# Layer 2's ELU goes through h's PSUM bank: g's two parts taken from there, and the order planned anew

## The chip, the cores and the metric

One Trainium2 chip, one core. The time is the device time of one execution in microseconds (us), on the slowest core, which here is the only one; lower is better. TensorE (PE), its weight loads (PEld), VectorE (DVE), ScalarE (ACT), GpSimd (POOL) and SyncE's DMA queue (SP) run beside each other and wait for one another by semaphores.

## What is computed

Three stages follow each other: an attention with hashed buckets, and two layers of a feed-forward network on its output.

```python
q_bucket, k_bucket = ...            # 6 sign bits of q @ proj, k @ proj
scores = scale * (q @ k.T), -1e9 where the buckets differ
attn = exp(scores - max) / (sum + 1e-9)
x = attn @ v                        # 16 heads x 768 x 64 -> 1536 tokens x 512
h = x @ w_in                        # layer 1, 512 -> 2048
g = h * tanh(softplus(h))           # Mish
x = g @ w_out                       # 2048 -> 512
h = x @ w2_in                       # layer 2, the same sizes
g = where(h > 0, h, exp(min(h, 0)) - 1)   # ELU
out = g @ w2_out
```

The weights reach the chip as 64 bit patterns and are turned into fp32 pairs there. Every product of the layers is made of three: each operand is split into a high part in fp32r and a low part, what is left, and high x high, high x low and low x high are summed in PSUM.

## The kernel before

**Attention.** 96 steps, 16 heads by 6 tiles of 128 queries. A step computes scores on PE (`st`), masks and takes the maximum on DVE (`pt`, L651), the exponential on ACT (L656), transposes on PE (`tu`, L707), splits the transposed part into `pth` (ACT, L712) and `ptl` (DVE, the helper `sub`, L353), and multiplies by v (`xt`, L720).

**Layers.** Tokens are columns: three blocks of 512 (`c` = 0, 1, 2). A layer is 32 tiles of weights (`w0` to `w31` and `w32` to `w63`; `u` counts them), in the order of `unit_orders`. "Up" products write h of one block into one PSUM bank, 12 matmuls each; "down" products read four tiles g and are added into `y_acc`, by ACT or by DVE (L1202). The first four up tiles are computed plainly (in layer 2: `h32_*` to `h35_*`), then the first down tiles follow (`h36_0`, `h37_0`, `h36_2` and so on, which read `g32` to `g35`, in this order). The other up tiles come in pairs, by seven products instead of eight (`pair_step`): results `h38_b1` to `h38_b4` for the outer blocks, and `h38_1c` and `h38_2c` for the middle one, each a bank; ACT copies `p` and DVE's additions at L957 join them. `turn` makes the sums of x that the pairs need, in `y_acc`, `T`, `x_hi` and `x_lo` (L1040 and the helpers), once for each layer, at its start; each of its additions and subtractions may run on DVE or on POOL.

**From h to g.** Each up tile goes from its bank to g, with `g.tile[:, 0]` its high part and `g.tile[:, 1]` its low part. Layer 1 (`mish`): ACT applies Mish in the bank, and `split` casts g's high part from the bank (ACT, the helper `copy`, L348) and subtracts it there (DVE, `sub`, L353). Layer 2 (`elu`, L893 to L904) has five instructions: relu of -h into a tile `gg` in SBUF (ACT, L896), the exponential of -gg in place (ACT, L898), max(gg - 1, h) into gg (DVE, L900), the cast of gg (ACT, L348) and the subtraction (L353), on DVE or POOL as the plan finds. The tiles `gg` are a ring of two (`NGG`).

**Weights.** `convert` turns a raw tile `wraw` into a weight pair: an ACT cast (L396), DVE's four instructions L398 (into a bank of their own, `c`), L401, L415, L418, and a cast and two or three sums and differences on ACT and POOL (L348, L353, L423, L432). In the attention the first ones run without that bank (L405, L410, L413, L415 on DVE). Seven PSUM banks go round among the h tiles, one belongs to `c`.

**What sets the order.** Nothing is scheduled by hand or while running: `Plan` lists every operation with a cost per engine, its inputs, its buffers and a priority, and gives each engine its sequence; the program then issues the instructions in that order. PE's sequence in the layers is fixed by the list of steps. Buffers of a ring are handed on in the plan's order. Tables of numbers (`EDGE`, `SHIFT`, `OFF`, `ODD`) shift the priorities of single operations; `pool` and `pool2` are the costs of an operation on POOL.

Of the kernel before, what the change touches and what calls it, by code (L numbers as in the profile page):

```python
# [30 lines left out]
def unit_orders():  # L31
# [25 lines left out]
EDGE = {}  # L57
SHIFT = {
# [78 lines left out]
def dve(n, fast=False):  # L137
    return 75 + (0.514 if fast else 1.028) * n


def act(n, psum=True):
    return (52 if psum else 95) + 0.833 * n


def pool(n):
    return 150 + 2.22 * n


def pool2(n):
    return 150 + 2.38 * n  # L150
# [144 lines left out]
def kernel(ctx, tc, qk, v, w, tab, out):  # L295
# [20 lines left out]
    def f32(t):  # L316
        return t.bitcast(F32)
# [983 lines left out]
```

## Time and profile before

| | |
|---|---|
| median of 3 runs | 739.52 us (739.17 to 742.06) |
| the profiled execution | 742.38 us, its span 740.6 us |
| granted clock of TensorE | 1.00 in all of the span (the 2.4 GHz level) |
| PE busy | 727.1 us, 98% |
| DVE busy | 579.4 us, 78% |
| ACT busy | 490.4 us, 66% |
| POOL busy | 423.2 us, 57% |
| time in the attention | to about 235 us, the layers from there on; layer 2 from about 480 us |

The page's busy times tell which engine can be the bound, the view of waits whom it waited for, and the timeline of a stretch what each engine did there, with the idle time ahead of a row and who ended it in square brackets. Line numbers are those of the kernel before; behind the change they are one higher up to the function `elu` and one lower behind it (L353 is L354 then, L900 is L901, L1040 is L1039).

### The profile page before, as it was taken

Reading aid. Unit: us, or ns where it says so; the run is one execution under the profiler, and the core shown is the slowest. Engines: PE = TensorE matmul, PEld = TensorE weight load, DVE = VectorE, ACT = ScalarE, POOL = GpSimd, SP = SyncE. Lnnn points to the kernel's source line nnn. Section 1 sums busy time; section 2 is a strip of 40 time slices with the busy share of each in tenths; the row PEclk is TensorE's granted clock in tenths of the full one; section 3 lists DMA queues with packets and bytes.
Section 4 is the critical chain, followed back from the end, with each engine's and each line's share of the span. In section 5 each row is a group of like instructions: output and inputs, shape, how many; then the busy total and the mean of one; then the engine's idle time right before and its main releaser. Section 6 shows DMA issues by size and latency. Waiting matters only on the chain. (4 is left out here: it accounts for less than half of the span.)

```text
span 740.6 us, 11709 instructions
## 1 busy us (share of the span) xinstructions
PE 727.1 (98%) x4083; PEld 639.0 (86%) x4083; DVE 579.4 (78%) x1065; ACT 490.4 (66%) x977; POOL 423.2 (57%) x359
## 2 busy tenths in 40 slices
PE   8999999999999999999999999999999999999998
PEld 7999999999898887888888888887788888888887
DVE  6899999999998979486577668999766785866672
ACT  5998998989997666554273457467766754844740
POOL 5427735734637886446446536866664755765640
PEclk9999999999999999999999999999999999999999
DMA  6875867777620302122112202212121121121112
GB/s 191 206 187 150 204 176 178 190 175 184 143 61 29 114 30 70 44 86 85 58 58 74 98 30 86 86 57 81 34 86 58 58 86 58 58 85 58 58 72 99
DMA packets 27498, 72.93 MB, mean 98 GB/s; under 512 B 6048, under 2 KB 8240, under 8 KB 27440
## 3 DMA queue, kind: packets, MB, share of 16 engines
q1 hardware_dynamic: 27296, 72.17, 34.3%
q8 instruction: 32, 0.52, 0.3%
q14 instruction: 26, 0.21, 0.1%
q10 hardware_dynamic: 144, 0.01, 0.0%
HBM read 45.76 MB, written 3.19 MB: 66 GB/s over the span
## 5 line engine op out<-in xcount | busy, mean ns | idle before, releaser
L848 PE MATMUL h<-g,w 128*128 128x512 f32 x1140 | 267.1, 390 | 3.0 <-DVE g L353 3.0
L848 PEld LDWEIGHTS h<-g,w 128*128 128x128 f32 x1140 | 212.6, 188 | 48.0 <-DVE g L353 4.1
L353 DVE TENSOR_TENSOR ptl<-tu,pth 128x512 fp32r<-128x512 f32 x144 | 97.5, 687 | 7.4 <-ACT pth L712 5.0
L651 DVE TENSOR_SCALAR_CACHE_REDUCE pt<-st 128x768 f32<-128x768 f32 x96 | 90.6, 948 | 5.7 <-PE st L648 5.4
L656 ACT ACTIVATE pt<-pt,nb 128x768 f32<-128x768 f32 x96 | 90.7, 945 | 3.6 <-DVE nb L654 3.4
L712 ACT CAST pth<-tu 128x512 fp32r<-128x512 f32 x144 | 82.2, 582 | 13.6 <-PE tu L707 12.7
L707 PE MATMUL tu<-ident,pt 128*128 128x128 f32 x576 | 85.9, 275 | 2.9 <-DVE ptl L353 2.8
L353 POOL TENSOR_TENSOR wt<-wt,w 128x512 f32<-128x512 f32 x40 | 52.8, 1320 | 62.1 <-DVE c L415 39.4
L1202 DVE TENSOR_TENSOR y_acc<-h,y_acc 128x512 f32<-128x512 f32 x71 | 48.8, 687 | 50.3 <-PE h L848 50.2
L648 PE MATMUL st<-qkt 76*128 76x384 f32 (+1 forms) x384 | 86.7, 350 | 0.8 <-DVE pt L651 0.8
L720 PE MATMUL xt<-pth,vt 128*128 128x256 f32 x288 | 79.3, 304 | 0.0
L707 PEld LDWEIGHTS tu<-ident,pt 128*128 128x128 f32 x576 | 67.4, 140 | 10.4 <-DVE ptl L353 6.2
L720 PE MATMUL xt<-ptl,vt 128*128 128x256 f32 x288 | 72.7, 281 | 0.0
L648 PEld LDWEIGHTS st<-qkt 76*128 76x128 f32 (+1 forms) x384 | 63.8, 191 | 1.7 <-DVE pt L651 1.7
L848 PE MATMUL h<-x_hi,w 128*128 128x512 f32 x192 | 60.5, 390 | 0.0
L348 ACT CAST w<-wt 128x512 fp32r<-128x512 f32 (+1 forms) x64 | 37.2, 583 | 33.0 <-DVE wt L401 18.0
L423 POOL TENSOR_TENSOR wt<-wt,ws 128x512 f32<-128x512 f32 x24 | 31.9, 1328 | 42.5 <-DVE ws L418 42.0
L432 POOL TENSOR_TENSOR w<-wt,ws 128x512 fp32r<-128x512 f32 x40 | 53.4, 1335 | 4.6 <-DVE ws L418 2.2
L720 PEld LDWEIGHTS xt<-ptl,vt 128*128 128x128 f32 x288 | 54.7, 190 | 0.1
L720 PEld LDWEIGHTS xt<-pth,vt 128*128 128x128 f32 x288 | 54.4, 189 | 0.0
L398 DVE TENSOR_SCALAR c<-ws 128x512 int32<-128x512 int32 x61 | 42.0, 689 | 14.3 <-ACT ws L396 12.7
L350 POOL CAST z<-rw 128x768 fp32r<-128x768 f32 x14 | 11.6, 826 | 64.0 <-DMA qkt<-z 41.7
(151 smaller groups left out, 1549.8 us busy)
## 6 DMA issues: line engine op xcount, KB each, us to landing
wraw<-in_w_dram SPq DMA_DIRECT2D x64, 512.0 KB
qkt<-z SPq DMA_DIRECT2D x30, 384.0 KB
rw<-in_qk_dram SPq DMA_DIRECT2D x16, 384.0 KB
qkt<-z SPq DMA_DIRECT2D x31, 192.0 KB
vr<-in_v_dram SPq DMA_DIRECT2D x8, 384.0 KB
out_dram<-y_acc SPq DMA_DIRECT2D x11, 256.0 KB
rr<-dr SPq DMA_DIRECT2D x14, 192.0 KB
xs<-xr SPq DMA_DIRECT2D x14, 192.0 KB
```

What stands on the lines that cost most here:

```text
L348: nc.scalar.copy(out=out, in_=in_)
L353: eng(e).tensor_tensor(out=out, in0=a, in1=b, op=ALU.subtract)
L398: o2 = p.op({DVE: dve(n)}, lambda e: nc.vector.tensor_scalar(out=bits(b), in0=bits(a), scalar1=3, scalar2=None, op0=ALU.logical_shift_left ...
L432: o9 = p.op({POOL: cost}, lambda e: nc.gpsimd.tensor_tensor(out=lo(), in0=t.tile, in1=s.tile, op=ALU.add), [o6, o8], [t, s, w_], prio)
L648: nc.tensor.matmul(st.tile[:, c, 0:HS], lhsT=wt.tile[0:n, q, t * 128:(t + 1) * 128], rhs=wt.tile[0:n, 2 + q, c * HS:(c + 1) * HS], start=( ...
L651: o = max_op = p.op({DVE: dve(S)}, lambda e: nc.vector.tensor_scalar(out=half(pt.tile), in0=st.tile[:, :, 0:HS], scalar1=-MASKED / SCALE, ...
L656: o = p.op({ACT: act(S, False) + 196}, lambda e: nc.scalar.activation(out=pt.tile, in_=pt.tile, func=AF.Exp, bias=nb.tile, scale=SCALE, ac ...
L707: nc.tensor.transpose(tu.tile[:, k, j], pt.tile[:, (2 * b + k) * 128:(2 * b + k + 1) * 128], ident)
L712: o = p.op({ACT: act(512)}, lambda e, tu=tu, ks=ks: nc.scalar.copy(out=hi.tile[:, ks], in_=flat(tu)), [o], [tu, hi], order(i, 'hi'))
L720: nc.tensor.matmul(xt.tile[:, 0:TH], lhsT=vt.tile[:, k, g % 2], rhs=m.tile[:, k], start=(k == 0 and j == 0), stop=(k == NKT - 1 and j == 1))
L848: nc.tensor.matmul(out(), lhsT=w_.tile[:, a, k], rhs=r, start=(start and n == 0), stop=(stop and n == 3 * len(ks) - 1), skip_group_check=True)
L1202: y = p.op({DVE: dve(n)}, lambda e, ya=ya, t=t, c=c: nc.vector.tensor_tensor(out=ya, in0=view(t.tile, c), in1=ya, op=ALU.add), [x, Y[m, c] ...
```

## The change

The maximum at L900 writes back into h's bank instead of gg; what follows is layer 1's `split`: the cast reads the bank (ACT), the subtraction reads the bank and runs on DVE. The two cost functions of POOL are given one new line, and the tables hold new numbers, so the whole order is planned anew.

```diff
-EDGE = {}
+EDGE = {'rr5': -12.0, 'rh#1': -1.0, ...
 SHIFT = {
-    'P1#0': -28, 'P1#1': -25.25, 'P1.1': -5, 'P1c#0': -20.5, 'P1c#1': 3.5, 'P1c.1': -22.75, 'P2#0': 19.5,
+    'P1#0': 41.25, 'P1#1': -121, 'P1.1': 37.5, 'P1c#0': 28.5, 'P1c#1': 53.75, 'P1c.1': -46.5, 'P2#0': -49.25,
...
 def pool(n):
-    return 150 + 2.22 * n
+    return 140 + 2.185 * n
 def pool2(n):
-    return 150 + 2.38 * n
+    return 140 + 2.185 * n
...
             a = p.op({DVE: dve(n)}, lambda e: nc.vector.scalar_tensor_tensor(
-                out=gg.tile, in0=gg.tile, scalar=1.0, in1=t.tile, op0=ALU.subtract, op1=ALU.max), [a], [t, gg], prio)
-            h = p.op({ACT: act(n, False)}, lambda e: copy(e, g.tile[:, 0], gg.tile), [a], [gg, g], prio)
-            return p.op({DVE: dve(n), POOL: pool2(n)} if BOTH else {POOL: pool2(n)}, lambda e: sub(
-                e, g.tile[:, 1], gg.tile, f32(g.tile[:, 0])), [h], [gg, g], prio, port=True)
+                out=t.tile, in0=gg.tile, scalar=1.0, in1=t.tile, op0=ALU.subtract, op1=ALU.max), [a], [t, gg], prio)
+            return split(t, a, prio, g)
```

**What moves between engines.** PE has 4085 instructions and ACT 884 in both; DVE goes from 971 to 986, POOL from 364 to 349. Layer 2's 48 subtractions were 22 on DVE and 26 on POOL and are all on DVE. Of the turns' work some goes the other way: of the 256 wide sums into `y_acc` DVE has 7 instead of 15, of the subtractions into `T` 15 instead of 20, of the 512 wide ones into `y_acc` 12 instead of 13, of those into `x_lo` 4 instead of 1. PE's order is the same in both layers; in the attention it differs for about steps 7 to 20 and for its last 30 us. The conversions of w0 and w1 that the attention hides are placed otherwise among DVE's rows: L410 of w0 three rows earlier, L415 of w1 eleven rows later.

**DVE, the start of layer 2, around g35_0's low part.** `gg...` is the ELU's buffer of the tile named behind it, `c39`, `wt39` and `ws39` are stages of the conversion of w39. Before:

```order
L900 SCALAR_TENSOR_TENSOR gg1252_6184<-gg1252_6184,h34_2_6146 128x512
L900 SCALAR_TENSOR_TENSOR gg1245_6171<-gg1245_6171,h35_0_6120 128x512
L398 TENSOR_SCALAR c39_6212<-ws39_6162 128x512
L401 SCALAR_TENSOR_TENSOR wt39_6217<-wraw39_6108,c39_6212 128x512
L415 TENSOR_SCALAR c39_6212<-wt39_6217 128x512
L418 SCALAR_TENSOR_TENSOR ws39_6162<-wraw39_6108,c39_6212 128x512
L353 TENSOR_TENSOR g34_2_6215<-gg1252_6184,g34_2_6215 128x512
L353 TENSOR_TENSOR g35_0_6219<-gg1245_6171,g35_0_6219 128x512
```

and of the change:

```order
L901 SCALAR_TENSOR_TENSOR h34_0_6109<-gg1238_6146,h34_0_6109 128x512
L402 SCALAR_TENSOR_TENSOR wt39_6160<-wraw39_6078,c39_6153 128x512
L416 TENSOR_SCALAR c39_6153<-wt39_6160 128x512
L354 TENSOR_TENSOR g34_0_6172<-h34_0_6109,g34_0_6172 128x512
L901 SCALAR_TENSOR_TENSOR h35_0_6136<-gg1245_6175,h35_0_6136 128x512
L419 SCALAR_TENSOR_TENSOR ws39_6150<-wraw39_6078,c39_6153 128x512
L354 TENSOR_TENSOR g35_0_6188<-h35_0_6136,g35_0_6188 128x512
```

The maximum writes h35_0's bank, one instruction of w39 stands between it and the subtraction instead of four, and g34_2 comes behind.

**ACT, the same place.** Before:

```order
L896 ACTIVATE gg1245_6171<-h35_0_6120 128x512
L896 ACTIVATE gg1252_6184<-h34_2_6146 128x512
L898 ACTIVATE gg1245_6171<-gg1245_6171 128x512
L348 CAST T1_0_3699<-y_acc_3696 128x256
L898 ACTIVATE gg1252_6184<-gg1252_6184 128x512
L348 CAST T2_0_3701<-y_acc_3696 128x256
L348 CAST x_hi_64<-y_acc_3696 128x512 x2
L348 CAST g34_2_6215<-gg1252_6184 128x512
L348 CAST g35_0_6219<-gg1245_6171 128x512
```

and of the change:

```order
L897 ACTIVATE gg1245_6175<-h35_0_6136 128x512
L899 ACTIVATE gg1245_6175<-gg1245_6175 128x512
L349 CAST T0_1_3698<-y_acc_3696 128x256
L349 CAST g35_0_6188<-h35_0_6136 128x512
L897 ACTIVATE gg1252_6201<-h34_2_6162 128x512
L349 CAST T1_1_3700<-y_acc_3696 128x256
L899 ACTIVATE gg1252_6201<-gg1252_6201 128x512
```

The tile's relu, exponential and cast stand with one other cast between them, and the next tile's relu behind its cast.

**DVE, the first pair of layer 2 (w38, w39), at its joined middle results.** Before:

```order
L900 SCALAR_TENSOR_TENSOR gg1405_6675<-gg1405_6675,h38_1c_6554 128x512
L398 TENSOR_SCALAR c45_6697<-ws45_6692 128x512
L900 SCALAR_TENSOR_TENSOR gg1412_6677<-gg1412_6677,h38_2c_6565 128x512
L401 SCALAR_TENSOR_TENSOR wt45_6712<-wraw45_6515,c45_6697 128x512
L415 TENSOR_SCALAR c45_6697<-wt45_6712 128x512
L418 SCALAR_TENSOR_TENSOR ws45_6692<-wraw45_6515,c45_6697 128x512
L353 TENSOR_TENSOR g38_1_6715<-gg1412_6677,g38_1_6715 128x512
```

and of the change:

```order
L901 SCALAR_TENSOR_TENSOR h38_1c_6556<-gg1405_6670,h38_1c_6556 128x512
L901 SCALAR_TENSOR_TENSOR h38_2c_6566<-gg1412_6676,h38_2c_6566 128x512
L399 TENSOR_SCALAR c44_6702<-ws44_6695 128x512
L354 TENSOR_TENSOR g39_1_6697<-h38_1c_6556,g39_1_6697 128x512
L354 TENSOR_TENSOR g38_1_6704<-h38_2c_6566,g38_1_6704 128x512
```

Both subtractions are DVE's now (g39_1's was POOL's) and stand behind one instruction of w44. The bank of h38_1c goes to h42_1c in both.

## Rows read from the trace of the kernel before

**Rows 1.** The page, busy time of each engine (share of the span) and instructions.

```profile
PE 727.1 (98%) x4083; PEld 639.0 (86%) x4083; DVE 579.4 (78%) x1065; ACT 490.4 (66%) x977; POOL 423.2 (57%) x359
```

**Rows 2.** Waits of PE: who waited for whom, us in total, times, longest.

```profile
PE h L848 <- DVE g L353: 3.0, 3, 1.4
PE tu L707 <- DVE ptl L353: 2.8, 3, 1.0
...
PE h_b L848 <- ACT p L348: 0.8, 1, 0.8
```

**Rows 3.** Busy time by stretch: length; PE, PEld, DVE, ACT, POOL; PEclk, DMA share, GB/s.

```profile
500.00:540.00 40.00, 37.35 (x163) 30.02 (x162) 32.69 (x49) 28.91 (x55) 25.26 (x21) 1.00 0.20 66
540.00:735.00 195.00, 195.00 (x977) 165.51 (x977) 130.99 (x205) 107.78 (x200) 113.19 (x98) 1.00 0.20 68
```

**Rows 4.** Timeline of PE, start of layer 2: start, us, instructions, [idle before, releaser].

```profile
518.34 5.75 PE L848 MATMUL h<-g,w 128*128 128x512 f32 x24 [1.29 <-DVE g L353]
525.45 1.90 PE L848 MATMUL h<-g,w 128*128 128x512 f32 x7 [1.36 <-DVE g L353]
```

**Rows 5.** Timeline of ACT, the same place.

```profile
508.72 1.08 ACT L896 ACTIVATE gg<-h 128x512 f32<-128x512 f32 x2
...
513.03 1.14 ACT L348 CAST g<-gg 128x512 fp32r<-128x512 f32 x2
516.70 0.60 ACT L896 ACTIVATE gg<-h 128x512 f32<-128x512 f32 x1 [2.54 <-DVE g L353]
```

**Rows 6.** Timeline of DVE, the same place.

```profile
515.92 2.36 DVE L353 TENSOR_TENSOR g<-gg,g 128x512 fp32r<-128x512 f32 x2
...
523.04 2.35 DVE L353 TENSOR_TENSOR g<-gg,g 128x512 fp32r<-128x512 f32 x2
```

**Rows 7.** Timeline of POOL, the same place.

```profile
516.08 1.66 POOL L423 TENSOR_TENSOR wt<-wt,ws 128x512 f32<-128x512 f32 x1 [0.84 <-DVE ws L418]
```

**Rows 8.** Groups of instructions, shapes apart: count | busy, mean ns of one | idle before.

```profile
L353 POOL TENSOR_TENSOR g<-gg,g 128x512 fp32r<-128x512 f32 x26 | 33.5, 1298 | 14.6 <-ACT g L348 14.6
L898 ACT ACTIVATE gg<-gg 128x512 f32<-128x512 f32 x48 | 30.4, 633 | 0.9
...
L957 DVE TENSOR_TENSOR h_b<-h_b,p 128x512 f32<-128x512 f32 x36 | 25.1, 696 | 14.1 <-PE h_b L848 11.0 <-ACT p L348 3.1
L353 DVE TENSOR_TENSOR g<-gg,g 128x512 fp32r<-128x512 f32 x22 | 20.6, 954 | 3.1 <-ACT g L348 2.7
L900 DVE SCALAR_TENSOR_TENSOR gg<-gg,h_b 128x512 f32<-128x512 f32 x24 | 16.5, 686 | 12.8 <-ACT gg L898 11.3 <-POOL w L432 1.5
L353 DVE TENSOR_TENSOR g<-h_b,g 128x512 fp32r<-128x512 f32 x24 | 16.5, 686 | 7.6 <-ACT g L348 7.6
...
L348 ACT CAST g<-h_b 128x512 fp32r<-128x512 f32 x24 | 14.2, 594 | 0.5 <-PE h L848 0.3
```

**Rows 9.** Timelines of POOL, DVE and PE in the attention, around 57 and 197 us.

```profile
54.88 1.84 POOL L757 TENSOR_TENSOR xr<-xr,xs 128x768 f32<-128x768 f32 x1
...
55.27 2.00 DVE L410 SCALAR_TENSOR_TENSOR wt<-wraw,wt 128x512 int32<-128x512 int32 x1
...
57.93 0.66 PE L707 MATMUL tu<-ident,pt 128*128 128x128 f32 x4 [0.98 <-DVE ptl L353]
...
194.61 1.98 DVE L415 TENSOR_SCALAR ws<-wt 128x512 int32<-128x512 int32 x1
...
197.70 0.66 PE L707 MATMUL tu<-ident,pt 128*128 128x128 f32 x4 [1.04 <-DVE ptl L353]
```

**Rows 10.** Timelines of DVE and PE where banks change hands, layer 1 and layer 2.

```profile
298.13 0.69 DVE L353 TENSOR_TENSOR g<-h_b,g 128x512 fp32r<-128x512 f32 x1
...
298.87 1.45 PE L848 MATMUL h<-g,w 128*128 128x512 f32 x5 [0.39 <-DVE g L353]
...
566.52 0.69 DVE L900 SCALAR_TENSOR_TENSOR gg<-gg,h_1c 128x512 f32<-128x512 f32 x1
...
569.53 0.28 PE L848 MATMUL h_1c<-x_hi,w 128*128 128x256 f32 x1
```

More of the change, by code (lines that the diff above doesn't have):

```diff
@@ L56 @@
 SEED, SPREAD = 0, 0.0
-EDGE = {}
+EDGE = {'rr5': -12.0, 'rh#1': -1.0, 'rh#2': -4.0, 'rh#3': 3.75, 'rh#13': -10.5, 'rh#14': 31.5, 'cp#1': 5.5, 'cp#3': 1.5, 'cp#14': -5.25, 'cp#15': 19.75, 'ld#1': -16.0, 'ld#2': -11.75, 'ld#13': -4.0, 'ld#14': 19.0, 'ld#15': 14.5, 'sp#1': -27.0, 'sp#2': -1.25, 'sp#13': -7.5, 'sp#14': -15.5, 'sp#15': -10.75, 'pj#2': -2.75, 'pj#3': -2.5, 'bits#2': -7.0, 'bits#3': -43.75, 'bits#13': 8.0, 'pc#2': 25.75, 'pc#3': 4.5, 'pc#13': 8.0, 'pc#14': -7.25, 'pc#15': -37.0, 'pb#1': -1.25, 'pb#2': 18.75, 'pb#3': 66.5, 'mk#1': 14.5, 'mk#2': 8.0, 'mk#3': 3.75, 'mk#13': -29.0, 'mk#14': 22.0, 'S0': 1.0, 'S1': 0.5, 'S2': 1.25, 'S4': 14.75, 'S6': -29.25, 'S7': -37.5, 'S8': -8.75, 'S9': -14.25, 'S10': -15.5, 'S87': -0.25, 'S88': 2.5, 'S90': 26.75, 'S91': 8.5, 'S92': -1.0, 'S94': 16.25, 'S95': 17.0, 'max0': -9.5, 'max1': 42.25, 'max2': 10.5, 'max3': -16.0, 'max5': -3.0, 'max6': 2.5, 'max7': -0.5, 'max8': 24.25, 'max9': 1.75, 'max10': -0.25, 'max11': -25.0, 'max12': -2.0, 'max84': -25.0, 'max85': 12.5, 'max86': 15.0, 'max87': -7.75, 'max88': 3.5, 'max89': -21.75, 'max93': -0.25, 'max94': -22.75, 'max95': 20.25, 'exp2': -1.75, 'exp3': -18.75, 'exp4': -8.5, 'exp5': -0.5, 'exp6': 14.5, 'exp7': 57.75, 'exp9': 2.0, 'exp10': 12.5, 'exp11': -3.0, 'exp12': -2.5, 'exp13': -11.25, 'exp86': -31.75, 'exp87': 4.0, 'exp88': -23.25, 'exp89': 3.0, 'exp90': 11.0, 'exp91': -0.25, 'exp92': -2.5, 'exp93': 7.0, 'exp94': 11.25, 'exp95': -11.0, 'sum5': -24.0, 'sum11': 1.5, 'sum87': 29.25, 'sum89': -7.0, 'sum93': 17.75, 'sum95': 6.5, 'eps5': -0.25, 'eps11': -4.75, 'eps85': -8.25, 'eps87': 14.75, 'eps89': -9.25, 'eps91': -20.25, 'eps93': -6.5, 'eps95': 48.0, 'T1': -12.75, 'T3': 10.75, 'T5': -29.75, 'T7': 28.75, 'T9': 7.75, 'T11': -8.0, 'T13': 1.0, 'T85': 8.75, 'T87': -21.75, 'T89': 8.5, 'T91': 8.0, 'T93': -0.5, 'T95': -11.5, 'hi3': 12.0, 'hi5': -0.25, 'hi7': 3.75, 'hi11': -63.0, 'hi13': -2.25, 'hi85': 21.25, 'hi87': 10.0, 'hi89': -10.25, 'hi91': 36.25, 'hi93': 4.25, 'hi95': 16.25, 'lo1': 3.75, 'lo3': -5.25, 'lo5': 13.5, 'lo7': 2.0, 'lo9': -8.75, 'lo11': -39.0, 'lo13': 4.0, 'lo85': -0.25, 'lo89': 27.25, 'lo91': -1.75, 'lo93': 17.0, 'lo95': -10.75, 'R91': -2.75, 'R93': -3.0, 'R95': 0.25, 'pv1': -4.25, 'pv11': 0.25, 'pv13': -0.25, 'pv85': 1.0, 'pv87': 11.5, 'pv91': 24.0, 'pv93': 11.75, 'pv95': 24.75, 'xc1': 19.0, 'xc3': -9.25, 'xc5': -52.75, 'xc7': -1.5, 'xc13': 3.75, 'xc85': -0.75, 'xc87': 42.75, 'xc89': -3.5, 'xc93': -0.5, 'xm5': -8.0, 'xm11': 8.0, 'rr11': 10.0, 'rh#15': 21.0, 'cp#2': 5.75, 'cp#13': 9.25, 'ld#3': -3.0, 'sp#3': 15.5, 'pj#1': -1.75, 'pj#13': 0.25, 'bits#1': -6.25, 'bits#14': 14.5, 'S13': -2.0, 'S86': 2.25, 'S89': 0.5, 'S93': 17.0, 'max4': 27.0, 'max91': -36.75, 'exp84': -2.0, 'sum85': 7.0, 'hi1': -16.25, 'hi9': -12.25, 'pv3': -1.75, 'pv5': -2.0, 'pv7': -0.25, 'pv9': 0.5, 'pv89': -28.25, 'xn11': 4.0}
@@ L131 @@
 WAIT = {'PE': 150, 'ACT': 0, 'DVE': 50, 'POOL': 50, 'SP': 100}
-OFF = {'rr': 41.5, 'rh': 63.5, 'cp': -137.25, 'ld': 2.0, 'sp': -1.25, 'pj': -5.75, 'bits': -149.5, 'pc': 18.0, 'pb': -54.0, 'mk': 208.25, 'v': 55.25, 'S': -1.5, 'max': -137.5, 'exp': 73.0, 'sum': 130.5, 'eps': 39.25, 'T': 11.25, 'hi': -16.75, 'lo': -121.5, 'R': 46.25, 'pv': 7.0, 'xc': 27.5, 'xa': -194.25, 'xn': -103.25, 'xh': -29.75, 'xm': 106.25}
-ODD = {'lo': [2.5, 0.0, 4.5, -89.5, 1.75, -25.0], 'T': [11.25, -11.5, 35.0, -11.25, 16.75, -10.0], 'pv': [7.25, -0.75, -0.5, -0.75, 16.0, -1.75], 'exp': [8.0, -86.0, -69.75, 0.25, -10.75, -1.0], 'hi': [-3.0, -2.0, 8.5, -1.0, -0.25, -7.5], 'S': [2.5, 1.25, 3.0, 0.0, 3.25, -1.25], 'xc': [2.75, -5.25, -4.25, -9.0, 0.0, 3.5], 'max': [1.75, 115.75, -2.0, 6.25, 6.0, 134.5]}
+OFF = {'rr': -9.0, 'rh': 17.75, 'cp': -38.25, 'ld': 7.5, 'sp': 0.75, 'pj': -5.75, 'bits': -198.5, 'pc': 91.0, 'pb': -170.0, 'mk': 182.25, 'v': -38.0, 'S': -1.0, 'max': -158.0, 'exp': 85.25, 'sum': 224.0, 'eps': -134.75, 'T': -51.25, 'hi': -10.25, 'lo': -225.25, 'R': 42.75, 'pv': 7.75, 'xc': 29.5, 'xa': 33.25, 'xn': -4.75, 'xh': -32.5, 'xm': -12.5}
+ODD = {'lo': [-18.0, 41.5, 21.5, -8.5, -9.25, 4.0], 'T': [-0.75, -36.5, -14.5, -7.0, 0.0, 14.5], 'pv': [0.0, 0.0, -4.25, -0.75, 0.0, -1.75], 'exp': [10.0, -81.0, -109.0, 33.25, -37.0, 43.25], 'hi': [2.0, 0.0, -98.75, 0.0, -4.25, 9.5], 'S': [2.5, 0.5, 3.5, 0.75, 2.5, -1.0], 'xc': [-0.5, 11.75, 2.0, -13.0, 6.0, -7.0], 'max': [-29.5, 1.0, -92.75, -2.0, 0.25, 0.0]}
 PE, ACT, DVE, POOL, SP = "PE", "ACT", "DVE", "POOL", "SP"
```

137 rows, old and new, of the table SHIFT are left out of this document.

## The prediction

> **What bounds the kernel now.** I read the page's busy times first: PE is busy for 727.1 of 740.6 us, 98% [rows 1]. So only PE's own waits, some 13 us, can be won by moving work between the other engines, and a change that leaves PE's instructions alone (it does, in both layers) is worth what it does to those waits. The view of waits on PE tells whom it waits for: the layers' products (L848) wait 3.0 us for a g part made by DVE at L353, three times, and the transposes of the attention (L707) wait 2.8 us for ptl, three times [rows 2]; the rest is under 1 us each, or lies in the first 20 us. Of the three, 0.39 us lies in layer 1 [rows 10], and 2.65 in layer 2. The table by stretches puts layer 2's share in one place: of the 40 us from 500 to 540, where its first products run, PE is busy for 37.35, and in the 195 us behind them for all 195.00 [rows 3]. The reader should see there too that the other engines aren't full: DVE has 32.69 of the 40 us, POOL 25.26.
>
> PE's timeline of that place shows two holes: 1.29 us before 518.34 and 1.36 us before 525.45, both released by DVE's L353 into g [rows 4]. Who was late? ACT's and DVE's rows tell the chain of g35_0. Its relu is the first of the pair at 508.72, its cast the second of the pair at 513.03, so g's high part stood at 514.17 [rows 5]. Its low part is the second subtraction of the pair at 515.92, which ended at 518.28, 0.06 us before PE went on [rows 6]. Two things lie between. DVE converted w39 first: four instructions stand ahead of the pair in its order. And the pair took 2.36 us, where two of 0.69 in a chain take 1.3 [rows 6, 8], beside a POOL instruction of 1.66 us at 516.08 [rows 7]. The next relu, at 516.70, had been held for 2.54 us until DVE's subtraction set a gg buffer free [rows 5]; that one and the next led to the pair at 523.04, which took 2.35 us [rows 6] and made the second hole. So the two holes have one cause: a ring of two gg buffers, each held over five instructions from relu to subtraction, and subtractions that read two SBUF tiles beside POOL.
>
> **The change, part by part.**
>
> *The maximum writes into the bank (L900).* No instruction is added. What it costs to write PSUM instead of SBUF isn't shown for this operation; the nearest row is the pair step's addition (L957), bank to bank, at 696 ns, against 686 for L900 into gg [rows 8]. So between 0 and +10 ns on each of 48; I take 0 and keep 0.5 us of DVE for the range, off PE's path.
>
> *The cast (ACT).* From a bank it took 594 ns in layer 1 [rows 8], from gg 1.14 us for a pair [rows 5], about the same. ACT, busy for 28.91 of 40 us where the layer starts [rows 3], hides it: worth nothing.
>
> *The subtraction.* Before, 22 ran on DVE at 954 ns and 26 on POOL at 1298 ns; now all 48 run on DVE out of a bank, for which layer 1 shows 686 ns [rows 8]. DVE: 48 x 0.686 - 22 x 0.954 = 32.9 - 21.0 = +11.9 us. POOL: 26 x 1.298 = 33.7 us less. Part of this is given back, since the plan hands some of the turn's additions from DVE to POOL. From 500 to 735 DVE is busy for 32.69 + 130.99 = 163.7 of 235 us [rows 3]; with 11.9 more it is 175.6, 75%. DVE has room, on average.
>
> *The ring.* A gg buffer is now free after the maximum, three instructions in, not five. ACT's new order shows what follows: relu, exponential and cast of one tile stand nearly side by side, where two relus and two exponentials stood ahead of both casts. I follow g35_0 through it by hand. Four products of 12 matmuls stand between the end of h35_0 and 514.63, where h36_0 starts; at 0.23 us a matmul (24 took 5.75, the last 0.39 of its own [rows 4, 8]) that is 4 x 2.76, so h35_0 ended at about 503.6. Relu 0.60, exponential 0.63, maximum 0.69, another cast and its own, 2 x 0.59, DVE's ws39 ahead and the subtraction, 2 x 0.69 [rows 5, 8]: 4.5 us, ready at about 508 if nothing stretches, 510 with one stretch and one queue of three. PE needs it for the fourth part of h36_0, 9 matmuls after 514.63, at 516.7. So 6 us to spare where 1.6 were missing. For g35_2 the product ends at about 509.1 and the need, with no hole ahead, is at 522.2; the chain again takes 4 to 7 us. Both holes close. What is late next is g34_1 and g35_1, whose products end at 511.9 and 514.6 against a need at 527.7.
> Worth: 1.29 + 1.36 = 2.65 us [rows 4]; if only one closes, 1.3.
>
> *The order planned anew.* PE's order is the same in both layers; in the attention it differs for about steps 7 to 20 and in the last 30 us. The tables hold no work, so this is worth only what the other PE waits do. The attention's two largest had the same cause: DVE's L410 took 2.00 us beside POOL's 1.84 us instruction of 54.88 and L415 took 1.98, each ahead of a ptl that PE then waited for, 0.98 and 1.04 us [rows 9]. The first began at 55.27, 1.45 us before POOL's ended, and took 1.31 us more than the 0.69 of L900, which is as long a tile [rows 8, 9]. The new order puts the first three DVE rows earlier and the second eleven later; whether a POOL instruction meets them there can't be read from an order. I take 0, with -2.0 (both go) and +2.0 (two more such meetings, 1.0 of PE's time each) as ends. The Trainium skill, "SBUF — State Buffer", section "Who interferes with whom", has GpSimd and VectorE share a pair of ports, which whoever comes first holds for its whole instruction, against a VectorE instruction that reads two SBUF tiles or runs in a two-port mode. By it a meeting can cost up to all of POOL's instruction, so 1.84 for each and +3.7 for two, not +2.0; this trace agrees in kind, and shows 1.31 of a possible 1.45. In layer 1 the wait of 0.8 us for ACT's copy p [rows 2] has w9's cast still ahead of it: 0, with -0.8 as the end. DVE converts w6 later there, and by hand w8 and w9 come only some 0.2 us ahead of their products, an estimate: one conversion instruction and a half late, +1, as the other end.
>
> *Sum.* The profiled execution took 742.38 us (its span 740.6 and 1.8 around it): 742.38 - 2.65 = 739.7. It stands 2.86 above the median of the three runs, 739.52; I forecast medians, so **736.9 us**, 0.36% less. A measurement of this kernel can tell about 0.5% (3.7 us) from no change.
>
> **The rivals.**
>
> *More goes than the two holes.* The same replanning also rids the attention of both meetings and layer 1 of its wait: 736.9 - 2.0 - 0.8 = 734.1. For it: one cause in both rows, and POOL loses 33.7 us of work. Against it: that work went in layer 2, not where the meetings are; the attention keeps its instructions.
>
> *New meetings.* The moved conversions meet POOL at two or three other places, 1.0 each by rows 9, or w8 and w9 are late by 1: 736.9 + 2 to 3 = 739 to 740.
>
> *A bank is held too long: slower.* Before, a bank was free after the maximum; now cast and subtraction hold it for 0.59 + 0.69 = 1.28 us more, plus what stands between them on ACT and DVE. PE, which writes its products into banks in a fixed order, then stands still. The tightest places are the pairs' joined products: h38_1c's maximum ran from 566.52 to 567.21, and h42_1c took that bank at 569.53 [rows 10], 2.3 us later. In the new order the second maximum and c44 lie between, and by hand the subtraction ends at about 569.2: 0.3 us to spare. There are six such pairs in the layer. If DVE's other work eats that 0.3 at each, the whole longer hold falls on PE: 6 x 1.28 = 7.7, and 736.9 + 7.7 = 744.6. It decides from the point where DVE's queue behind the second maximum holds over 0.3 us. For it: layer 1 has this form already, and there PE waited 0.39 us until 298.87 to start h8_1, for the bank whose subtraction ran from 298.13 to 298.82 [rows 10]. Against it: that was the one such wait among layer 1's 48 tiles [rows 2], and the new order puts the subtractions at once behind the maxima or one instruction later.
>
> *The change doesn't reach the holes.* DVE has 48 of the subtractions to do where it had 22, and at the layer's start it is already at 82%; if the weights' conversions push g35_0 and g35_2 back as far as before, the time stays at 739.5. Against it: the 6 us to spare above.
>
> **How the numbers follow.** Forecast (735.5 to 738): 0.41. More goes (732.5 to 735.5): 0.27. New meetings (738 to 741): 0.15. Not reached: 0.07. Bank held (741 to 746): 0.10. Faster by over 0.5% means below 735.8: all of the second case and a fifth of the first, 0.27 + 0.08 = 0.35. Slower means above 743.2: most of the bank's case, 0.09 with a little of the third. The rest, 0.56, is within 0.5%. The range 733.0 to 741.2 leaves out the lowest fifth of the second case (0.05), the bank's (0.10) and a little of the third (0.02); it takes in the bounds of the ring (1.3 to 2.65), of the attention (-2.0 to +2.0) and of layer 1 (-0.8 to +1).
>
> **What would show it.** The view of waits on PE has no g by DVE over 0.5 us, and the stretch from 500 to 540 shows PE busy for about 40 us. ACT's relu into gg is no longer released by DVE's subtraction. L901's maximum takes 680 to 700 ns and the 48 subtractions out of h about 685, with none near 954; POOL's busy time falls by some 25 to 34 us. Right about the rivals: DVE's ptl again in PE's waits with 2 us or more (new meetings); PE released by a subtraction into g at a product that does not read g, an h_1c, h_2c or h_b (bank held). I am wrong if PE's wait at the layer's start remains, or if the time falls by more than 6.5 us, which PE's waits behind the first 20 us don't hold.

## The result, and the profile after

The changed kernel takes **747.25 us** (median of 4 runs, 746.55 to 748.52) against 740.42 us before (4 runs beside it, 739.17 to 742.06): ratio 1.009, interval 1.0071 to 1.011. It is slower by 0.9%, where 0.36% faster was forecast. The profiled execution took 748.52 us, its span 746.7, so 6.1 us more than before's, and these 6.1 us are followed here.

Waits of PE after the change (to be held against [rows 2]):

```profile
PE h_b L849 <- ACT p L349: 7.0, 2, 6.4
...
PE tu L708 <- DVE ptl L354: 0.8, 1, 0.8
...
PE h L849 <- DVE y_acc L1201: 0.3, 1, 0.3
```

The line that led before, h waiting for a g part from DVE, is gone. In its place stands one wait of 6.4 us for ACT's copy p. The table by stretches says where (length; PE, PEld, DVE, ACT, POOL; clock, DMA share, GB/s):

```profile
280.00:300.00 20.00, 13.60 (x48) 10.63 (x47) 15.09 (x21) 13.11 (x26) 14.76 (x17) 0.83 0.17 52
287.00:293.00 6.00, 5.30 (x13) 4.14 (x14) 4.65 (x7) 3.40 (x7) 5.92 (x7) 0.50 0.40 113
...
500.00:540.00 40.00, 40.00 (x178) 33.10 (x178) 35.02 (x53) 30.66 (x60) 27.05 (x26) 1.00 0.20 66
540.00:735.00 195.00, 194.06 (x968) 163.83 (x967) 139.57 (x228) 108.50 (x204) 83.53 (x77) 1.00 0.19 65
```

The start of layer 2 is full now, 40.00 of 40 us against 37.35 [rows 3], as forecast. The loss lies in layer 1, in the 20 us from 280, where PE is busy for 13.60 us and the granted clock averages 0.83; from 287 to 293 it is 0.50, the 1.2 GHz level. None of the five instructions that the ELU consists of runs there. PE's timeline, after the change:

```profile
278.71 0.73 PE L849 MATMUL h_b<-x_hi,w 128*128 128x512 f32 x2 [0.54 <-POOL w L354]
...
287.70 5.49 PE L849 MATMUL h_b<-T,wa 128*128 128x512 f32 x12 [6.40 <-ACT p L349]
292.99 0.58 PE L849 MATMUL h_b<-x_hi,wb 128*128 128x512 f32 x1
...
294.56 1.77 PE L849 MATMUL h<-g,w 128*128 128x512 f32 x7
```

and before:

```profile
280.79 2.88 PE L848 MATMUL h_b<-T,wa 128*128 128x512 f32 x12
284.52 0.50 PE L848 MATMUL h_b<-x_hi,wb 128*128 128x512 f32 x1 [0.84 <-ACT p L348]
...
286.01 2.88 PE L848 MATMUL h<-g,w 128*128 128x512 f32 x12
```

The same 12 matmuls, the first six of which add into the bank that the copy p6_01 saves, start at 287.70 instead of 280.79: 6.91 us later. They then take 5.49 us instead of 2.88: the granted clock is at its lower level behind a wait of 6.4 us. To the start of the next product it is 5.29 us, against 2.89 to the end of before's row and its wait (284.52 - 0.84 - 280.79), which is 2.40 more. Before's own wait of 0.84 us for p6_02 doesn't come up. 6.91 + 2.40 - 0.84 = 8.47 us late, and 284.52 + 8.47 = 292.99.

**The ledger**, by the starts of the same matmul in both traces: 0.55 us ahead where layer 1 starts (the attention won a little); 8.5 late behind the rows above; 8.0 late where layer 2 starts (before's wait of 0.39 for a bank [rows 10] is gone too); 6.4 late behind the place of the first hole and 4.75 behind the second, so both closed and gave 3.3 back; 6.0 late behind the rest of layer 2, mostly by two waits near the end (0.60 us for p at 666.90, 0.28 for a bank at 684.05, and what starting again costs); 6.1 at the end.

Why was p6_01 late? ACT's timeline, before:

```profile
275.86 0.67 ACT L396 ACTIVATE ws<-wraw 128x512 f32<-128x512 f32 x1 [0.63 <-POOL wa L353]
277.11 0.67 ACT L396 ACTIVATE ws<-wraw 128x512 f32<-128x512 f32 x1 [0.58 <-POOL wb L353]
278.06 0.62 ACT L348 CAST w<-wt 128x512 fp32r<-128x512 f32 x1 [0.29 <-DVE wt L401]
279.12 0.41 ACT L348 CAST T<-y_acc 128x256 fp32r<-128x256 f32 x1 [0.43 <-DVE y_acc L1040]
279.63 0.59 ACT L348 COPY p<-h_b 128x512 f32<-128x512 f32 x1
...
283.57 0.41 ACT L348 CAST x_hi<-y_acc 128x256 fp32r<-128x256 f32 x1 [0.43 <-DVE y_acc L1040]
...
285.27 0.40 ACT L348 CAST T<-y_acc 128x256 fp32r<-128x256 f32 x1
...
287.41 0.41 ACT L348 CAST T<-y_acc 128x256 fp32r<-128x256 f32 x1 [1.25 <-DVE y_acc L1040]
```

and after:

```profile
282.00 0.40 ACT L349 CAST T<-y_acc 128x256 fp32r<-128x256 f32 x1
282.89 0.67 ACT L397 ACTIVATE ws<-wraw 128x512 f32<-128x512 f32 x1 [0.48 <-POOL wa L354]
283.46 0.39 ACT L349 CAST x_hi<-y_acc 128x256 fp32r<-128x256 f32 x1
284.91 0.41 ACT L349 CAST T<-y_acc 128x256 fp32r<-128x256 f32 x1 [1.07 <-DVE y_acc L1039]
285.23 0.67 ACT L397 ACTIVATE ws<-wraw 128x512 f32<-128x512 f32 x1
286.24 0.62 ACT L349 CAST w<-wt 128x512 fp32r<-128x512 f32 x1 [0.35 <-DVE wt L402]
286.76 0.40 ACT L349 CAST T<-y_acc 128x256 fp32r<-128x256 f32 x1
287.07 0.58 ACT L349 COPY p<-h_b 128x512 f32<-128x512 f32 x1
```

Look first at the turn's three narrow casts, x_hi and two T. They run at nearly the same times in both, 283.57, 285.27 and 287.41 against 283.46, 284.91 and 286.76. They aren't later: p6_01 moved. Before, it stood ahead of all three, right behind T's cast at 279.12; now it stands behind them, with six rows between T's cast and it. ACT ran its rows in the order of the program, so a copy that PE waited for sat behind three casts that PE didn't wait for. The 6.40 us are 1.10 to the end of T's cast at 282.40, 4.67 of the six rows, and 0.63 of the copy.

The three others of the six rows are casts of w8 and w9, and these are later. Before, they stood ahead of p6_01 too, at 275.86, 277.11 and 278.06; now they run at 282.89, 285.23 and 286.24, 7 to 8 us later. Behind this stands w6: the last of DVE's four instructions for it ran at 261.21 before and at 273.59 after, and POOL's sums that need it came later as well. w6's low part held PE for 0.54 us at 278.71, and w8's first cast waited for wa at 282.89. w8's second cast ended at 286.86, only 0.2 us ahead of p6_01's start. By these rows the weights alone would have held the copy almost as long.

PE also needs w8 itself soon after. Its low part on POOL, before:

```profile
280.32 1.28 POOL L432 TENSOR_TENSOR w<-wt,ws 128x512 fp32r<-128x512 f32 x1
```

and after:

```profile
289.00 1.28 POOL L433 TENSOR_TENSOR w<-wt,ws 128x512 fp32r<-128x512 f32 x1
```

The first matmul that reads it is the third in the last row of PE's timelines above; before, it started at 286.47. After the change the low part ends at 290.28. So in this order PE would have stood there, some 3.8 us late, even with p6_01 in time: an estimate from these rows, which the copy's wait hides.

### The profile page after: what moved, and what is told of

Read it like the earlier page. It is cut to its first block, busy times and chain, and to the rows that moved or that the text cites. A ratio compares the mean times of both kernels' runs of the same rounds, so it can differ in the third digit from the quotient of the medians.

```text
span 746.7 us, 11667 instructions
## 1 busy us (share of the span) xinstructions
PE 730.1 (98%) x4083; PEld 640.3 (86%) x4083; DVE 586.2 (79%) x1080; ACT 485.8 (65%) x977; POOL 396.7 (53%) x344
## 5 line engine op out<-in xcount | busy, mean ns | idle before, releaser
L397 ACT ACTIVATE ws<-wraw 128x512 f32<-128x512 f32 x61 | 40.6, 673 | 8.3 <-POOL wa L354 4.4
```

The source lines that it names most:

```text
L397: o1 = p.op({ACT: act(n, False)}, lambda e: nc.scalar.activation(out=a.tile, in_=high().bitcast(F32), func=AF.Copy, scale=2.0 ** -112), [l ...
```

## The experiments

Before took 741.0 to 741.1 us (median of 11 to 23 runs) beside these kernels; each ratio is against the runs of before on the same chip. Two questions: is the loss the new order's or the new ELU's, and in the order, is it the place of p6_01 or the lateness of what it waits behind?

**The new ELU alone, under before's tables and costs** (layer 2 is planned anew by itself, the layers ahead stay):

```diff
...
+                out=t.tile, in0=gg.tile, scalar=1.0, in1=t.tile, op0=ALU.subtract, op1=ALU.max), [a], [t, gg], prio)
+            return split(t, a, prio, g)
```

> The kernel before with the new ELU alone (its tables and its POOL costs stay; the planner still places layer 2 anew, what comes ahead of layer 2 hardly moves). Theory A, that the loss lies in the new tables at the start of layer 1: about 737.5 us (736 to 739), PE's wait for g between 515 and 530 gone (2.65 us in the kernel before), layer 1 as in the kernel before, clock 1.00. Theory B, that the ELU through the bank costs itself (bank held longer, DVE fuller): 743 or more, with waits of PE in layer 2. Theory C, that a loss is spread over the whole new order: 737 to 739 too.

Measured: 742.56 us, 1.0021 of before (1.0006 to 1.0036). No loss in layer 1, and both holes are gone; yet it is a little slower and misses the 737.5 us expected, for other waits came up in layer 2. Its table by stretches:

```profile
500.00:540.00 40.00, 40.00 (x178) 33.04 (x177) 30.50 (x48) 27.35 (x53) 26.27 (x26) 1.00 0.20 67
540.00:735.00 195.00, 192.22 (x958) 161.92 (x958) 132.82 (x219) 102.69 (x195) 77.34 (x72) 1.00 0.19 65
```

The 2.65 us won at the layer's start are lost behind it: PE is busy for 192.22 of 195 us there, where before was busy for all [rows 3]. ACT's timeline at one of these places shows the same pattern as in layer 1:

```profile
633.98 0.62 ACT L348 CAST w<-wt 128x512 fp32r<-128x512 f32 x1 [2.72 <-DVE wt L401]
634.51 0.58 ACT L348 COPY p<-h_b 128x512 f32<-128x512 f32 x1
```

ACT stood idle for 2.72 us ahead of a weight's cast, for DVE's half of the conversion, with p behind it; PE's product that waits for this p starts at 635.14, held for 0.58 us by it. Near 698.5 the same cost 1.04.

**The new order alone, with the old ELU** (the changed kernel, its ELU as before):

```diff
-                out=t.tile, in0=gg.tile, scalar=1.0, in1=t.tile, op0=ALU.subtract, op1=ALU.max), [a], [t, gg], prio)
-            return split(t, a, prio, g)
+                out=gg.tile, in0=gg.tile, scalar=1.0, in1=t.tile, op0=ALU.subtract, op1=ALU.max), [a], [t, gg], prio)
...
```

> The changed kernel with the old ELU (gg in SBUF, subtraction on DVE or POOL), the new tables and POOL costs kept. Theory A: layer 1's start as in the changed kernel, PE waits about 6.4 us for ACT's copy p near 281 to 288 and the clock falls behind it: 747 to 752, as the holes at layer 2's start may come back. Theory B: the loss is gone, about 740.

Measured: 749.76 us, 1.011 (1.0096 to 1.0124). PE's timeline:

```profile
286.06 4.50 PE L849 MATMUL h_b<-T,wa 128*128 128x512 f32 x12 [6.43 <-ACT p L349]
...
523.99 0.50 PE L849 MATMUL h<-g,w 128*128 128x512 f32 x1 [2.09 <-ACT g L349]
525.15 15.16 PE L849 MATMUL h<-g,w 128*128 128x512 f32 x59 [0.66 <-DVE g L354]
```

The wait in layer 1 is there without the new ELU, and with the old ELU there are holes in layer 2 as well, of 2.09 and 0.66 us. So the loss is the order's. Within this order the new ELU is worth 747.25 - 749.76 = -2.5 us by the medians, and -1.9 us if each is held against its own runs of before (740.42 and 741.07). That is near the forecast's 2.65, but the intervals of the two ratios overlap.

**Only the cost functions of POOL** (before with their new numbers, tables and ELU as they were):

```diff
-    return 150 + 2.22 * n
+    return 140 + 2.185 * n
...
-    return 150 + 2.38 * n
+    return 140 + 2.185 * n
```

> The kernel before with the two new cost functions of POOL alone (lower by 0.03 to 0.11 us for 512 columns), so planned anew with the old tables. Theory A: the new costs alone move operations, and any order that puts PE's copies behind late sums of the turn loses some us, in the attention or at layer 1's start: 741 to 750, most likely a few us lost at layer 1's start. If the costs do nothing by themselves: 740.5.

Measured: 751.09 us, 1.0134 (1.0119 to 1.0148). Two cost functions, smaller by up to 8%, plan everything anew and lose 10 us. PE's timeline, in the same place of layer 1:

```profile
285.02 4.52 PE L848 MATMUL h_b<-T,wa 128*128 128x512 f32 x12 [2.58 <-ACT p L348]
```

The same copy is late again, by 2.58 us and behind the same three casts, and the clock falls behind that too. Here w8's and w9's casts come early. Much of the rest is waiting for g where layer 2 starts, 2.30 and 1.65 us.

**Before, with p6_01 behind the three casts** (three dependencies more for the copy; the plan places the rest around it):

```diff
-                st["p1"] = save(1, [])
+                st["p1"] = save(1, [] if part else AHEAD[:])
+                AHEAD.clear()
...
+                        if (kind, part, j) == (0, 1, 0) and i != 1:
+                            AHEAD.append(h)
```

> The kernel before with the copy p6_01 put behind the same three casts (T1_0, T2_0, x_hi, 256 wide), its only change. Theory A: PE waits at the seventh product of layer 1's first pair until T2_0's cast and the copy are done, by rows of the kernel before about 286.5 instead of 280.8, so 4 to 6 us, and runs below full clock behind it: 745 to 750 us. If the place on ACT is not the cause: about 740.5.

Measured: 748.8 us, 1.0094 (1.0078 to 1.0109), with old ELU and old tables. ACT's timeline:

```profile
286.55 0.40 ACT L348 CAST T<-y_acc 128x256 fp32r<-128x256 f32 x1 [1.86 <-DVE y_acc L1042]
286.86 0.58 ACT L348 COPY p<-h_b 128x512 f32<-128x512 f32 x1
```

and PE's:

```profile
287.49 5.49 PE L848 MATMUL h_b<-T,wa 128*128 128x512 f32 x12 [7.23 <-ACT p L348]
```

Up to this copy the sequences are before's, and w8's cast is as early as there. So 7.2 us of waiting and the half rate behind it come out of before by this one place in ACT's sequence: it is enough for the whole loss of layer 1.

**The changed kernel, with those casts and the first ones of w8 and w9 behind p6_01:**

```diff
...
+                for o in BEHIND if not part else ():
+                    o.after.append(st["p1"])
+                    st["p1"].next.append(o)
+                    o.left += 1
...
+                        if (kind, part, j) == (0, 1, 0) and i != 1:
+                            BEHIND.append(h)
```

> The changed kernel with three of layer 1's 256 wide casts of the turn (T1_0, T2_0, x_hi) and the first casts of w8 and w9 put behind the copy p6_01 in the plan. Theory A: PE's wait for p6_01 falls from 6.4 us to under 2 and the clock stays at 1.00; w8 may be 1 to 2 us late instead: 739 to 743 us. A rival, that the turn's chain over POOL and DVE is what binds, so that PE waits for its results instead: 745 or more.

Measured: 748.07 us, 1.0083 (1.0069 to 1.0097): nothing won, and not the 739 to 743 expected. The plan put another cast in the same place, the narrow one of T2_1. ACT's timeline:

```profile
285.79 0.40 ACT L349 CAST T<-y_acc 128x256 fp32r<-128x256 f32 x1 [3.82 <-DVE y_acc L1048]
286.10 0.58 ACT L349 COPY p<-h_b 128x512 f32<-128x512 f32 x1
```

**The same, with that cast behind p6_01 too:**

```diff
-                        if (kind, part, j) == (0, 1, 0) and i != 1:
+                        if (kind, part) == (0, 1) and (i == 4 or j == 0 and i != 1):
```

> As p6_free, with T2_1's 256 wide cast behind the copy p6_01 too, which had taken the place of the other three. Theory A (ACT stands in its order at a cast of the turn whose sums are late, and the copy behind it is what PE needs): p6_01 is copied at about 282.3, PE goes on at about 283 instead of 287.7, the clock stays at 1.00; p6_02 and w8 come late in turn, 2 to 3 us together: 742 to 744.5 us. If PE then waits as long for the turn's or the weights' results: 746 or more.

Measured: 746.26 us, 1.0078 (1.006 to 1.0096), about 1 us less than the change and in the range of the rival, that PE waits for other results instead. PE's timeline:

```profile
282.39 3.02 PE L852 MATMUL h_b<-T,wa 128*128 128x512 f32 x12 [1.66 <-ACT p L349]
288.31 0.50 PE L852 MATMUL h_b<-x_hi,wb 128*128 128x512 f32 x1 [2.90 <-ACT p L349]
...
293.03 2.59 PE L852 MATMUL h<-g,w 128*128 128x512 f32 x10 [1.37 <-POOL w L435]
```

p6_01 came at 281.76 and PE went on at 282.39, 5.3 us earlier than after the change. Then p6_02 was 2.90 us late behind the same casts, and w8's low part 1.37. Of the 6.4 us most came back one product later, so the changed order is behind in more than one place here: the copy's place is enough for the loss, but setting it right doesn't undo it, as the weights are late too. What it would take to mend all of them within this order wasn't tried.

**Before's layer 1 with the new tables for layer 2** (a second table `SHIFT2`, the change's numbers, used for operations of the pairs, turns, up and down tiles of layer 2, with the new ELU; then also for the conversions from w36 on):

```diff
...
+            second = u != "" and self.cls not in ("cv", "ld", "sm") and int(u) >= 1
...
-            second = u != "" and self.cls not in ("cv", "ld", "sm") and int(u) >= 1
+            second = u != "" and self.cls != "ld" and int(u) >= (36 if self.cls in ("cv", "sm") else 1)
```

> The kernel before with the new ELU; for layer 2's products, turn and ELU the table SHIFT of the changed kernel, for all else (attention, layer 1, weights) that of the kernel before. Theory A: no loss in layer 1, holes at layer 2's start closed, and the new waits of the ELU alone (2.5 us for p, 1.3 for g in the middle of layer 2) smaller where the new table fits the new ELU: 738 to 741 us. If the new waits come with the ELU whatever the table: 742 to 743 as with the new ELU alone.

> As hybrid2, with the table of the changed kernel for the weights' conversions of layer 2 from w36 on too. Theory A: 738 to 741 us, nearer to layer 2 of the changed kernel, which was 2 us shorter than before. If the new waits come with the ELU whatever the table: 742 to 743.

Measured: 749.75 us, 1.0112 (1.0096 to 1.0129), and 748.3 us, 1.011 (1.008 to 1.0139). Both miss the 738 to 741 expected. That the numbers of a table fit only the order in which they were found would explain it, but isn't shown. Layer 1 lost nothing in either. In both, PE stood for 3.63 us at one of layer 2's first products; in the first:

```profile
486.25 0.50 PE L924 MATMUL h<-x_lo,w 128*128 128x512 f32 x1 [3.63 <-POOL x_lo L429]
```

**Five instructions moved by hand.** If the cost is queue places, it should go away without any new planning. The kernel with the new ELU alone keeps its whole order, but five instructions are issued a little later: the casts of w9, w53 and w61 on ACT behind the copies p6_02, p50_01 and p58_01, and on DVE L410 of w0 and L415 of w1 behind the ptl that PE waited for [rows 9].

```diff
+PAIRS = (("p6_02", "9"), ("p50_01", "53"), ("p58_01", "61"))
...
+        for o in find(DVE, "wraw0", "wt0")[1:2]:
+            later(o, ptl(o))
+        for o in find(DVE, "wt1", "ws1")[1:2]:
+            later(o, ptl(o))
+        for p, w in PAIRS:
...
+                later(cast, o)
```

> The kernel before with the new ELU alone (742.6 us in its own run), whose issue order is changed at five places and nowhere else: three copies p (p6_02 in layer 1, p50_01 and p58_01 in layer 2) stand ahead of the weight's cast that ACT waited at, and two of DVE's conversions (L410 of w0, L415 of w1) stand behind the next ptl. Theory A (a wait of PE there is one instruction's place in an in-order queue ahead of it): the five waits of PE, 1.0 + 0.7 + 1.2 + 1.3 + 1.2 us, go: 737 to 738.5 us, faster than both kernels. Rival (the work ahead is late in any order, so PE waits for the next result instead): 741 to 743.

Measured: **739.72 us** (12 runs, 739.0 to 740.36) against 741.02 (23 runs): 0.9984 (0.9975 to 0.9993). It is the one version here that is faster than both kernels clear of its interval, by 0.16% against before, and by the medians some 7.5 us faster than the change. The 737 to 738.5 expected are missed by 1.2 us. ACT's timeline at the place shown above:

```profile
631.37 0.59 ACT L377 COPY p<-h_b 128x512 f32<-128x512 f32 x1 [1.22 <-PE h_b L877]
632.87 0.62 ACT L377 CAST w<-wt 128x512 fp32r<-128x512 f32 x1 [0.91 <-DVE wt L430]
```

p is now released by PE, whose bank it copies, and the cast comes behind it in time. In the table by stretches layer 2 reads:

```profile
500.00:540.00 40.00, 40.00 (x178) 33.04 (x177) 29.58 (x46) 28.12 (x55) 26.73 (x26) 1.00 0.23 74
540.00:735.00 195.00, 193.30 (x974) 163.50 (x974) 133.92 (x220) 101.67 (x194) 76.34 (x71) 1.00 0.19 65
```

193.30 against 192.22: what is left are mostly waits of 0.89 us for g at 576 and 0.36 for a joined result at 701. PE's wait for ptl fell from 3.0 us in three to 0.8 in one, beside a new one of 0.7 for nb. The move of w9 won nothing: p6_02 then stood behind the narrow cast of x_hi, and PE waited 0.8 us for it as before; its wait for a bank of layer 1 [rows 10] grew to 0.89 us, with this move in both kernels that have it.

**The same three moves that before has room for, with the old ELU** (w9, L410, L415):

> The kernel before with the old ELU and three of these five places changed (p6_02, L410 of w0, L415 of w1; the other two waits it doesn't have). Theory A: three waits of PE go, 1.0 + 1.1 + 1.2 us: 737.5 to 739 us, with the two holes at layer 2's start as in the kernel before. Rival: 740.5 to 741.5.

Measured: 739.98 us (12 runs), 0.9993 (0.9982 to 1.0005): not told apart from before by its interval, and above the 737.5 to 739 expected. The holes of layer 2 stay. Against it the new ELU with its two other moves is 0.26 us faster by the medians, which is within the noise of both. So no run here shows that the 2.65 us of the two holes come off the whole time.

## Why the prediction was wrong

By the ledger the 6.1 us are -0.55 in the attention, +8.6 in layer 1, -3.3 at the two holes and +1.3 in the rest of layer 2. The level was off as well: the forecast starts from 739.52, the median of three runs, where longer series put before at 741.0 to 741.1.

*The two holes.* Right, and by the steps given: one cause, a ring held too long. Forecast -2.65, measured -3.3 in the ledger; so each of the two cost some 0.3 us more than the idle time in its row. A part of that is how idle time is counted: from the end of a matmul, 0.39 us behind its start, where the next one would have started 0.23 behind it. The groups after the change, shapes apart:

```profile
L354 DVE TENSOR_TENSOR g<-h_b,g 128x512 fp32r<-128x512 f32 x48 | 32.8, 684 | 12.2 <-ACT g L349 12.2
...
L901 DVE SCALAR_TENSOR_TENSOR h_b<-gg,h_b 128x512 f32<-128x512 f32 x24 | 16.6, 692 | 4.3 <-ACT gg L899 4.0
...
L897 ACT ACTIVATE gg<-h 128x512 f32<-128x512 f32 x12 | 7.2, 597 | 0.0
```

Subtractions from a bank take 684 ns (686 forecast), the maximum into a bank 692 against 686 into gg [rows 8], within the 0 to 10 ns allowed. The relu of the layer's first tiles waits for nothing; before, DVE's subtractions held these 12 for 4.5 us.

*POOL and DVE.* POOL's busy time fell from 423.2 [rows 1] to 396.7 us, by 26.5 where 25 to 34 were forecast. DVE rose by 6.8 only.

*The bank held too long.* Not seen. No wait of PE in layer 2 ends at a subtraction into g; the one bank that came late (0.28 us at 684.05) was held for an addition into y_acc.

*The attention.* Taken at 0, it won 0.55 us, within the ends given: two of three waits for ptl went, 2.0 us, and smaller waits for pt and others came.

*The rest of layer 2.* It had no term beyond the bank's, and lost 1.3 us: a wait of 0.60 us for p and the 0.28 for a bank, with what starting again costs.

*The order planned anew, layer 1.* **This is the step that failed**: "the wait of 0.8 us for ACT's copy p has w9's cast still ahead of it: 0, with -0.8 as the end ... +1, as the other end". The term measured +8.6 (from 0.55 ahead to 8.0 late): 6.4 of a wait and 2.4 of a slower clock, with small ones on both sides. The wait was for another copy, p6_01. It made no wait before, so it wasn't in the rows from which I started, and I followed only the copy that was already late. But the new order holds it: on ACT p6_01 stands behind the three casts of the turn that it stood ahead of. The time could be estimated from rows of before, too. The last of the casts it was moved behind ran there at 287.41; the matmuls that need p started at 280.79. Add the cast's 0.41 and the copy's 0.59, and PE stands until about 288.4, 7.6 us later, an estimate from these rows. The measured shift is 6.9, and 7.23 us of waiting with that move alone. The step was argued with "the tables hold no work, so this is worth only what the other PE waits do", which leaves out the waits that a new order makes.

The other end of the term, and the rival "New meetings", had weights late by 1 us, where w8 and w9 were put some 0.2 us ahead of their products. The sign was right and the size wrong: w8's low part is some 3.8 us late by the rows above. Its wait doesn't show in the trace, since PE stands for p6_01 first. What each of the two would cost alone in this order isn't shown.

Meetings of DVE and POOL have a part in layer 1, too. DVE's timeline after the change, ahead of the casts:

```profile
280.79 2.35 DVE L1039 TENSOR_TENSOR y_acc<-y_acc 128x256 f32<-128x256 f32 x2 [3.27 <-POOL y_acc L1039]
283.06 1.49 DVE L354 TENSOR_TENSOR T<-y_acc,T 128x256 fp32r<-128x256 f32 x1
284.47 0.41 DVE L1039 TENSOR_TENSOR y_acc<-y_acc 128x256 f32<-128x256 f32 x1
```

A sum that takes 0.41 us alone took some 1.2 in the pair at 280.79, while POOL ran instructions of 1.45 us, and T1's cast waited for the last of these rows. How much of the 6.4 us would go without that stretching wasn't tried; the narrow casts were no earlier before the change, so for these casts it doesn't explain the difference between the kernels. The Trainium skill, "SBUF — State Buffer", section "Who interferes with whom", calls the shared pair of ports an exclusive lock; these rows agree in kind.

## What to carry to other kernels

A new order of in-order queues isn't worth "only what the present waits do". Go through every short instruction that the bounding engine waits for, find its place on its engine in the old and the new order, and price each row that it is moved behind by the time at which that row's inputs come, not by its duration. Include the copies that weren't late before, and see whether the weights still come in time. Then move the few instructions that are in the way, and leave the plan alone: in this kernel all eight versions planned anew, and the change itself, were slower than before, by 1.5 to 10 us, while five instructions moved by hand won 2.8 us on the kernel with the new ELU alone, which puts it 1.3 us below before.

## What the runs showed of the hardware

A long wait of PE costs more than itself. Behind waits of 6.4, 6.43 and 7.23 us the same 12 matmuls took 5.49, 4.50 and 5.49 us instead of 2.88, and behind one of 2.58 us still 4.52. Behind one of 1.66 us they took 3.02, and before's waits of 0.8 to 1.4 us left the granted clock of their stretch at 1.00. In the changed kernel that is 2.4 us on top of 6.4, and it isn't in the view of waits.
